# A Mamba-2 scan with an FFN on one core: increments of two pairs ahead of the state sums, two products ahead of y, and three unread products

## Chip, cores and metric

The kernel runs on one core of a Trainium2 chip. The metric is the device time in microseconds (us) of one execution; a number of executions give a median. Lower is better.

## What is computed

Two parts follow each other. The first is a Mamba-2 scan over 4 batches, 8 heads and 768 steps, in chunks of 32 in the reference; the second is a feed-forward layer over the 3072 rows of 256 that the scan gives.

```python
for c in range(nc):                       # scan, for each batch and head
    cum = np.cumsum(log_a[chunk])
    M = (C @ B.T) * exp(cum_i - cum_j) * causal
    y = M @ x + (C @ state) * exp(cum)
    state = exp(sum(la)) * state + sum_j B_j x_j exp(cum_last - cum_j)
h = y_rows @ w_in                         # 3072 x 256 by 256 x 2048
g = h / (1 + exp(-1.702 * h))
out = g @ w_out                           # 2048 x 256
```

All of it is in fp32. The weights come as 64-bit floats and are turned to fp32 in the kernel with integer and float operations (`fields`, `clamp`, `rounded`, `join`; `narrow` calls several of them).

## The kernel before

The 3072 rows are taken in six groups of 512. A group is two *pairs* (`p`), a pair is two stretches of 128 steps, and each such stretch has two sides of 64 steps; the kernel's chunk is one side. For a pair the scan does this:

- `decay` (VectorE) makes the decays L and the weighted B, Be; `turn_only` transposes B and C on TensorE into a PSUM bank `tp`, and ScalarE copies them out; `since_start` (VectorE, L546) makes CsT from the bank `tp`.
- `gain` (TensorE, L591) makes the four increments of the state of each pair in two PSUM banks, A0 and A1, that both pairs of a group share.
- `keep` (VectorE) first spreads a pair's increments out of A into the tile S (two operations, L610), and then adds the states up from side to side (up to four operations, L622), each of which reads the one before.
- `score` (TensorE, L560) makes C times B in the area `cb`; `weigh` (VectorE, L571) multiplies it into L.
- `finish` (TensorE) makes y: products of state and CsT (L649), products of L and x (L670), and the other state products. A tiny POOL operation stands between the first and the second set of state products. ScalarE then copies y out to yT (L694).

The scan of one group is woven into the feed-forward work of the one before. Group 0's hidden layer and projection are plain products: `half` (L729) and `hidden` (L715) make h, and `project_all` (L829) sums the output over 16 blocks, with other work given to it at numbered places: `at(in_project[0], 7, ...)` runs ahead of block 7's four products. From group 1 on both layers use seven products for 2 x 2 blocks instead of eight. A first-layer block j is written `j.1` to `j.7` (L787 into a bank X, L797 into a bank Y), `j.D` is VectorE's addition out of Y and the copies of X (L906), `j.S` and `j.T` are ScalarE's activations, and `j.3` needs `j.D` to have read Y. An additional VectorE addition follows `j.3`. `P` is one second-layer product into `acc` (L888). Second-layer products need mixes of the weights (`mix_w`, VectorE, L854) and of the activations (`mix_g`, L755).

The order on each engine is the order of the program text: `in_order` ties every instruction to the one before it on its engine. [...] PSUM banks come from a pool of four (`bank`), taken in turn: a new bank waits until the last reader of the one four before it is done. So Y of block 2 takes the bank that A0 had, and X and Y of the next blocks follow in turn. The tiles S come from a pool of three. SP issues nearly all transfers, in program order as well: the loads of later pairs (`load`), the spread of their decays (`spread`) and the stores.

In the first scan, `half(1, 0)` is the second set of hidden products of pair 0; it waits for a piece of `w_in` that VectorE joins (`join(1)`, L194). `half(0, 1)` is the first one of pair 1; it waits for yT. Between them on TensorE stands pair 1's y. VectorE's joins in turn wait for ScalarE's `clamp` (L172, L173), and ScalarE does these after its copy of y.

Of the kernel before, what the change touches and what calls it, by code (L numbers as in the profile page):

```python
# [16 lines left out]
P = 128  # L17
# [18 lines left out]
def kernel(  # L36
# [31 lines left out]
    nc = tc.nc  # L68
# [9 lines left out]
    NC = S // P  # L78
# [6 lines left out]
    PG = CG // 2  # L85
# [81 lines left out]
    def clamp(i):  # L167


        e = power[i]  # L170
        z = e.bitcast(FP32)
        nc.scalar.activation(z, e, AF.Relu, scale=-8.0, bias=edge[:, 0:1])  # L172
        nc.scalar.activation(e, z, AF.Relu, scale=-1.0, bias=edge[:, 1:2])  # L173
# [37 lines left out]
    def spread(p):  # L211

        if p - 2 in ra:
            ra[p] = ra[p - 2]
        else:
            ra[p] = words(f"a{p}").bitcast(FP32)[:, :2 * NH * H].rearrange(
                "p (k e) -> p k e", k=2)
        b, c = divmod(2 * p, NC)
        for i, side in enumerate(SIDES):
            nc.sync.dma_start(  # L220
                out=ra[p][side],
                in_=scratch[b, c:c + 2, i].rearrange("c h i -> c (h i)").unsqueeze(
                    0).to_broadcast([H, 2, NH * H]))
# [39 lines left out]
    ones = const.tile([P, P], FP32, name="ones")  # L263
# [33 lines left out]
    for k in range(2):  # L297
        t = cum[:, 2 * k:2 * k + 2].rearrange("p c s -> p (c s)")

        nc.vector.tensor_tensor_scan(  # L300
            out=t, data0=carry[:, 2 * k:2 * k + 2].rearrange("p c s -> p (c s)"), data1=t,
# [13 lines left out]
    def pick_a(p):  # L315
# [17 lines left out]
        out=same, in_=same, pattern=[[-N, NH], [0, D]], compare_op=ALU.is_ge,  # L333
        fill=0.0, base=0, channel_multiplier=1)
    nc.gpsimd.affine_select(
        out=same, in_=same, pattern=[[N, NH], [0, D]], compare_op=ALU.is_ge,
        fill=0.0, base=N - 1, channel_multiplier=-1)
# [7 lines left out]
        out=part, in_=same[:, :, 0].rearrange("p (r q) -> p q r", q=Q), op=ALU.add, axis=AX.X)  # L345
# [202 lines left out]
    def score(pairs, to=None):  # L548

        cb = (area(f"cb{pairs[0]}") if to is None else to).rearrange(  # L550
            "p r (k e) -> p r k e", k=2 * PG)
        for n, p in enumerate(pairs):
            s = st[p]
            BT, CT = s.pop("BT"), s.pop("CT")
            s["cb"] = cb[:, :, 2 * n:2 * n + 2]
            for k in range(2):
                for i, side in enumerate(SIDES):
                    for r in range(R):
                        rows = slice(32 * r, 32 * r + 32)
                        nc.tensor.matmul(  # L560
                            out=s["cb"][side, r, k].rearrange("p (q i) -> p q i", q=Q),
                            lhsT=BT[rows, k, side], rhs=CT[rows, k, :, side],
                            start=True, stop=True, tile_position=(32 * r, H * i),
                            skip_group_check=True)

    def weigh(p, ks=(slice(0, 2),)):

        Lv = Ls[p].rearrange("p k r q i -> p k r (q i)")
        cb = st[p]["cb"].rearrange("p r k e -> p k r e")
        for k in ks:  # L570
            nc.vector.tensor_tensor(out=Lv[:, k], in0=Lv[:, k], in1=cb[:, k], op=ALU.mult)  # L571
# [3 lines left out]
    def last_chunk(p, m):  # L575

        return (4 * p + m + 1) % (2 * NC) == 0

    def gain(pairs):

        A = [bank(f"A{pairs[0]}_{i}")[:, :2 * len(pairs) * Q * D].rearrange(
            "p (k e) -> p k e", e=Q * D) for i in range(2)]
        for n, p in enumerate(pairs):
            Be = BE.pop(p)
            for k in range(2):
                for r in range(R):
                    heads = slice(Q * r, Q * r + Q)
                    for i, side in enumerate(SIDES):
                        if last_chunk(p, 2 * k + i):
                            continue  # L590
                        nc.tensor.matmul(  # L591
                            out=A[i][32 * r:32 * r + 32, 2 * n + k],
                            lhsT=Be[side, k, heads].rearrange("p h n -> p (h n)"),
                            rhs=rx[p][side, k, heads].rearrange("p h d -> p (h d)"),
                            start=True, stop=True, tile_position=(H * i, 32 * r),
                            skip_group_check=True)
            increment[p] = [t[:, 2 * n:2 * n + 2] for t in A]

    def keep(p, ms=range(4)):

        b, c = divmod(2 * p, NC)
        if 0 in ms:
            state[p] = ssd.tile([P, 4, HB * D], FP32, tag="S", name=f"S{p}", bufs=3)
        new = state[p]
        ms = [m for m in ms if not last_chunk(p, m)]
        for i in range(2):
            ks = [m // 2 for m in ms if m % 2 == i]
            if ks:
                k, n = ks[0], len(ks)
                nc.vector.tensor_tensor(  # L610
                    out=new.rearrange("p (k s) (b e) -> p s k b e", s=2, b=HB // Q)[
                        :, i, k:k + n],
                    in0=increment[p][i][:, k:k + n].unsqueeze(2).to_broadcast(
                        [P, n, HB // Q, Q * D]),
                    in1=own.rearrange("p (b q) d -> p b (q d)", q=Q).unsqueeze(1).to_broadcast(
                        [P, n, HB // Q, Q * D]), op=ALU.mult)
        for m in ms:
            if 2 * c + m > 0:
                k, i = divmod(m, 2)
                old = new[:, m - 1] if m else state[p - 1][:, 3]  # L620
                e = i * H + H - 1
                nc.vector.scalar_tensor_tensor(  # L622
                    out=new[:, m], in0=old, scalar=since[b][:, c + k, e:e + 1],
                    in1=new[:, m], op0=ALU.mult, op1=ALU.add)
# [92 lines left out]

        nc.scalar.activation(gT[g, j][:, i], h, AF.Silu, scale=GELU_SCALE)

    def half(j, t):  # L720

        if t == 0:
            block(0, j)
        h = bank(f"h0_{j}_{t}").rearrange("p (i e) -> p i e", i=2)
        cols = slice(t * HT, (t + 1) * HT)
        for i in range(2):
            f = 2 * j + i
            for k in range(NK):
                nc.tensor.matmul(out=h[:, i], lhsT=w_in[:, k, f * P:(f + 1) * P],  # L729
                                 rhs=yT[0][:, k, cols] if t else early_y[:, k],  # L730
                                 start=(i == 0 and k == 0), stop=(i == 1 and k == NK - 1),
                                 skip_group_check=True)
        nc.scalar.activation(gT[0, j][:, :, cols], h, AF.Silu, scale=GELU_SCALE)
# [283 lines left out]
    keep(1, (0,))  # L1017
    join(1)
    keep(1, (1, 2))
    half(1, 0)  # L1020
    weigh(1)
    load(PG)
    spread_rows(1)
# [6 lines left out]
    def at(places, i, *work):  # L1030
        places.setdefault(i, []).extend(work)
# [10 lines left out]
    for i, k in ((2, 1), (3, 3), (4, 4), (5, 6)):  # L1042
# [13 lines left out]
    at(in_project[0], 2, lambda: clamp(8), lambda: decay(PG + 1), lambda: clip_rows(1),  # L1056
       lambda: decay_rows(1), lambda: turn(PG + 1))
    at(in_project[0], 4, lambda: narrow(8))
    at(in_project[0], 6, lambda: clamp(9), lambda: gain(pairs))
    at(in_project[0], 7, lambda: score(pairs), lambda: keep(PG), lambda: keep(PG + 1),  # L1060
       lambda: weigh(PG), lambda: weigh(PG + 1))
    at(in_project[0], 9, lambda: narrow(9))
    at(in_project[0], 11, lambda: finish(pairs))
# [4 lines left out]
    for k, i in enumerate((9, 13)):  # L1068
# [4 lines left out]

    later = n, n + 1
    at(after, "H0", lambda: decay(n), lambda: decay(n + 1), lambda: turn(n), lambda: turn(n + 1))
    at(after, "H1", lambda: gain(later), lambda: score(later), lambda: keep(n),
       lambda: keep(n + 1), lambda: weigh(n), lambda: weigh(n + 1), lambda: spread(3 * PG))
    assert [b for b in range(NB) if 3 * CG <= b * NC < 4 * CG] == [2]


    for f in range(NF):
        if f >= 4:
            hidden(0, f)
        elif f % 2:
            half(f // 2, 1)
        for do in in_hidden[0].get(f, []):
            do()
    project_all(0, in_project[0])
# [8 lines left out]
    def run(g, steps, products=(), **do):  # L1097


        products = iter(products)  # L1100
        for step in steps.split():
            if step == "P":
                product(*next(products))
            elif step in do:
                do[step]()
            else:
                j, i = step.split(".")
                first(g, int(j), i)
        assert next(products, None) is None
# [11 lines left out]
    def ahead(g, p=None):  # L1121

        pairs = (p, p + 1) if p else ()
        for k in pairs:
            turn_only(k)
        if pairs:
            gain(pairs)
        for k in pairs:
            since_start(k)
        mix_y(g)  # L1130
        for k in pairs:
            keep(k)

    def more_loads():
        load(p + 1)
        spread(p + 1)

    run(1, "2.1 3.1 2.5 2.6 3.6 2.2 2.7 3.5 3.7 3.2 2.D 2.4 3.D 3.4 2.S 3.S y L 2.3 2.T 3.3 3.T",
        y=lambda: finish(later), L=more_loads)
    mix_w(0)  # L1140
    for j in range(2):
        mix_g(1, j)
    run(1, "4.1 P P 4.6 P P 4.7 P 4.5 P 4.2 P 4.D", seven(1, 0))
# [97 lines left out]
```

## Time and profile before

| what | us |
|---|---|
| median of 4 runs | 370.53 (370.14 to 370.73) |
| the profiled execution, its time | 370.6 |
| the profiled execution, its span from the first to the last instruction | 368.8 |
| TensorE busy | 359.4 |
| VectorE busy | 251.0 |
| ScalarE busy | 150.7 |

The chain of work that ended last is, by the page, TensorE for 75% of the span and VectorE for 11%. A TensorE product of fp32 is two records in the trace, each with a weight load of its own. Here is the timeline as the profile tells it: the first scan lies in the first 25 us, group 0's hidden layer ends at about 52 us and its projection at about 87 us, with the scan of group 1's pairs inside it (A at 62.9, y at 74.4). Group 1's first hidden blocks follow, then A of group 2's pairs at 94.4 and their y at 102.6. From about 108 us on, both layers' products stand close together, and the scans of later groups stand between them (y at 160.5, 216.8 and 273.0).

A timeline line reads: start, length, engine, line and operation, what it writes and reads, how many instructions were merged, and in brackets the idle time ahead of it on its engine with what ended it ("issue" where the profile shows nothing that it waited for).

### The profile page before, as it was taken

How to read it: one execution, taken by the hardware profiler on the slowest of the kernel's cores; microseconds unless marked ns; L12 is line 12 of the kernel's file. 1: busy time of each engine (PE TensorE's matmuls, PEld its weight loads, DVE VectorE, ACT ScalarE, POOL GpSimd, SP SyncE). 2: the span in 40 equal slices, each digit the busy share in tenths (PEclk: the TensorE clock that was granted, in tenths of full speed). 3: DMA queues.
4: the chain of work that ended last, by engine and by line, in shares of the span. 5: the costliest groups of instructions: out<-in, count | busy, mean ns of one | idle time of the engine just before them, and what ended most of it. 6: DMA issues, size and time to landing. Idle time of an engine off the chain costs nothing.

```text
span 368.8 us, 8716 instructions
## 1 busy us (share of the span) xinstructions
PE 359.4 (97%) x3734; PEld 309.0 (84%) x3734; DVE 251.0 (68%) x472; ACT 150.7 (41%) x341; POOL 12.0 (3%) x42
## 2 busy tenths in 40 slices
PE   8989999999999999999999999999999999999995
PEld 4764468886679999889999989999988999989995
DVE  5989979997738999568577466577474355374353
ACT  5759553212442333444333444333435331453320
POOL 4310000000000000000000000000000000000000
PEclk9999999999999999999999999999999999999999
DMA  9997689045863210076200052000010000010001
GB/s 152 220 367 128 210 190 146 4 127 107 147 107 47 63 38 2 2 140 91 59 2 2 0 103 73 0 2 2 1 60 2 0 3 0 2 57 2 0 2 57
DMA packets 86029, 25.03 MB, mean 68 GB/s; under 512 B 76136, under 2 KB 79464, under 8 KB 85992
## 3 DMA queue, kind: packets, MB, share of 16 engines
q1 hardware_dynamic: 83544, 24.09, 29.7%
q10 hardware_dynamic: 2448, 0.39, 0.6%
q8 instruction: 29, 0.48, 0.6%
q14 instruction: 8, 0.07, 0.1%
HBM read 21.23 MB, written 3.24 MB: 66 GB/s over the span
## 4 chain that ended last, share of the span: by engine, by line
PE 75%; DVE 11%; issue 8%; SPq 2%; DMA 1%; ACT 1%; POOL 0%; ACTq 0%; DVEq 0%
PE acc L888 31%; PE X L787 16%; PE Y L797 12%; PE o L829 5%; PE y L649 3%; PE y L670 2%; PE h L715 2%; DVE p L188 2%; SPq L123 2%; PE cb L560 1%; DVE m L177 1%; PE tp L514 1%; DVE p L161 1%; PE A L591 1%; DVE m L164 1%
## 5 line engine op out<-in xcount | busy, mean ns | idle before, releaser
L888 PEld LDWEIGHTS acc<-mw,mg 128*128 128x128 f32 x480 | 67.5, 191 | 4.2
L888 PE MATMUL acc<-mw,mg 128*128 128x128 f32 x480 | 69.2, 275 | 0.0
L792 ACT ACTIVATE ac<-X 128x256 f32<-128x256 f32 x76 | 29.1, 383 | 81.1 <-PE X L787 80.6
L906 DVE TENSOR_TENSOR gT<-Y,ac 128x512 f32<-128x512 f32 x38 | 26.1, 690 | 48.7 <-PE Y L797 36.0
L764 ACT ACTIVATE gT<-gT 128x512 f32<-128x512 f32 (+1 forms) x76 | 39.4, 520 | 36.4 <-DVE gT L906 35.8
L888 PEld LDWEIGHTS acc<-w_out,gT 128*128 128x128 f32 x320 | 44.1, 191 | 2.5
L787 PE MATMUL X<-my,mi 128*128 128x256 f32 x152 | 45.7, 383 | 0.1
L888 PE MATMUL acc<-w_out,gT 128*128 128x128 f32 x320 | 45.2, 275 | 0.0
L906 DVE TENSOR_TENSOR gT<-Y,b 128x256 f32<-128x256 f32 x38 | 16.0, 421 | 34.4 <-PE Y L797 34.3
L829 PE MATMUL o<-w_out,gT 128*128 128x256 f32 x128 | 28.8, 381 | 0.0
L715 PE MATMUL h<-yT,w_in 128*128 128x512 f32 x64 | 28.5, 595 | 0.2 <-DVE w_in L194 0.2
L755 DVE TENSOR_TENSOR mg<-gT 128x512 f32<-128x512 f32 x40 | 27.3, 682 | 0.0
L829 PEld LDWEIGHTS o<-w_out,gT 128*128 128x128 f32 x128 | 23.9, 190 | 3.4 <-issue 0.2
L787 PEld LDWEIGHTS X<-my,mi 128*128 128x128 f32 x152 | 24.2, 191 | 1.7 <-ACT ac L792 0.3
L888 PEld LDWEIGHTS acc<-mw,gT 128*128 128x128 f32 x160 | 23.0, 191 | 2.2 <-DVE mw L854 0.4
L888 PE MATMUL acc<-mw,gT 128*128 128x128 f32 x160 | 24.4, 277 | 0.0
L888 PEld LDWEIGHTS acc<-w_out,mg 128*128 128x128 f32 x160 | 23.1, 191 | 1.4
L888 PE MATMUL acc<-w_out,mg 128*128 128x128 f32 x160 | 24.0, 275 | 0.0
L715 PEld LDWEIGHTS h<-yT,w_in 128*128 128x128 f32 x64 | 11.8, 190 | 14.1 <-issue 12.2
L797 PE MATMUL Y<-my,mi 128*128 128x256 f32 x76 | 22.8, 382 | 0.6 <-DVE S L610 0.5
L787 PE MATMUL X<-yT,w_in 128*128 128x256 f32 x76 | 22.9, 385 | 0.1
L787 PE MATMUL X<-my,w_in 128*128 128x256 f32 x76 | 22.8, 384 | 0.0
(137 smaller groups left out, 524.4 us busy)
## 6 DMA issues: line engine op xcount, KB each, us to landing
a<-scratch SPq DMA_DIRECT2D x18, 256.0 KB
bits<-in_moe_w_out_dram SPq DMA_DIRECT2D x4, 1024.0 KB
x<-in_x_dram SPq DMA_DIRECT2D x24, 128.0 KB
out_dram<-c SPq DMA_DIRECT2D x9, 256.0 KB
bits<-in_moe_w_in_dram SPq DMA_DIRECT2D x4, 512.0 KB
bits<-in_moe_w_in_dram SPq DMA_DIRECT2D x2, 1024.0 KB
b<-in_B_dram SPq DMA_DIRECT2D x24, 64.0 KB
c<-in_C_dram SPq DMA_DIRECT2D x22, 64.0 KB
```

Source lines behind the costliest of these rows:

```text
L123: (queue if dst is rc else nc.sync).dma_start(out=dst[p][:, k], in_=src[b, :, sl, :].rearrange("h s d -> s h d"))
L188: nc.vector.scalar_tensor_tensor(out=p2, in0=hi, scalar=0x80000000, in1=p2, op0=ALU.bitwise_and, op1=ALU.bitwise_or)
L649: nc.tensor.matmul(out=y[i][:, t, 2 * n + k], lhsT=old[rows], rhs=st[p]["CsT"][rows, k, SIDES[i]], start=begin(i, range(HB)), stop=False, ...
L715: nc.tensor.matmul(out=h, lhsT=w_in[:, k, f * P:(f + 1) * P], rhs=yT[g][:, k], start=(k == 0), stop=(k == NK - 1))
L755: nc.vector.tensor_tensor(out=t[:, 0:2], in0=B[:, :, 1], in1=B[:, 0], op=ALU.subtract)
L764: nc.scalar.activation(o, i, AF.Silu, scale=GELU_SCALE)
L787: nc.tensor.matmul(out=s["X"], lhsT=lhsT, rhs=rhs, start=i == "1", stop=i == "4", skip_group_check=True)
L792: nc.scalar.activation(copy, s["X"], AF.Copy)
L797: nc.tensor.matmul(out=o, lhsT=lhsT, rhs=rhs, start=s.pop("new", False), stop=i != "5", skip_group_check=True)
L829: nc.tensor.matmul(out=o[k // 2][:, k % 2], lhsT=gT[g, f // 2][:, f % 2, k * P:(k + 1) * P], rhs=w_out[:, f], start=(f == 0 and k % 2 == 0 ...
L888: nc.tensor.matmul(out=acc[g][0][i][:, cols], lhsT=h[:, cols], rhs=w, start=(j == 0 and i in (0, 2, 5, 6) and k == 0), stop=(j == NF // 2 ...
L906: nc.vector.tensor_tensor(out=o, in0=v, in1=w, op=ALU.add)
```

## The change

Five edits. `keep` is split into `part_of` (the increments out of A) and `add_up` (the sums), and `keep_both` does the first for both pairs and then the second for both. It takes the place of two calls of `keep` in group 0's projection, after group 1's first hidden blocks, and in `ahead`. `gain(pairs)` moves in group 0's projection from place 6 to place 7, so four products of block 6 now come before it. In group 1's first stretch, products `2.3` and `3.3` and the activations after them come ahead of `y`, and `mix_w(0)` goes from the end of that stretch to a place ahead of `2.3`. `half` can put products of ones into its own bank ahead of its real ones, which overwrite them: two ahead of `half(1, 0)`, one ahead of `half(0, 1)`. The operations that are computed and read are the same; the order on TensorE, VectorE and ScalarE changes, that on POOL and SP does not.

```diff
--- before.py
+++ after.py
@@ -598,7 +598,17 @@
 
     def keep(p, ms=range(4)):
 
-        b, c = divmod(2 * p, NC)
+        part_of(p, ms)
+        add_up(p, ms)
+
+    def keep_both(pairs):
+
+        for p in pairs:
+            part_of(p, range(4))
+        for p in pairs:
+            add_up(p, range(4))
+
+    def part_of(p, ms):
         if 0 in ms:
             state[p] = ssd.tile([P, 4, HB * D], FP32, tag="S", name=f"S{p}", bufs=3)
         new = state[p]
@@ -614,8 +624,12 @@
                         [P, n, HB // Q, Q * D]),
                     in1=own.rearrange("p (b q) d -> p b (q d)", q=Q).unsqueeze(1).to_broadcast(
                         [P, n, HB // Q, Q * D]), op=ALU.mult)
+
+    def add_up(p, ms):
+        b, c = divmod(2 * p, NC)
+        new = state[p]
         for m in ms:
-            if 2 * c + m > 0:
+            if 2 * c + m > 0 and not last_chunk(p, m):
                 k, i = divmod(m, 2)
                 old = new[:, m - 1] if m else state[p - 1][:, 3]
                 e = i * H + H - 1
@@ -717,12 +731,16 @@
 
         nc.scalar.activation(gT[g, j][:, i], h, AF.Silu, scale=GELU_SCALE)
 
-    def half(j, t):
+    def half(j, t, fill=0):
 
         if t == 0:
             block(0, j)
         h = bank(f"h0_{j}_{t}").rearrange("p (i e) -> p i e", i=2)
         cols = slice(t * HT, (t + 1) * HT)
+
+        for i in range(fill):
+            nc.tensor.matmul(out=h[:, i], lhsT=ones, rhs=ones.unsqueeze(1).to_broadcast([P, 2, P]),
+                             start=True, stop=True, skip_group_check=True)
         for i in range(2):
             f = 2 * j + i
             for k in range(NK):
@@ -1017,7 +1035,7 @@
     keep(1, (0,))
     join(1)
     keep(1, (1, 2))
-    half(1, 0)
+    half(1, 0, 2)
     weigh(1)
     load(PG)
     spread_rows(1)
@@ -1056,8 +1074,8 @@
     at(in_project[0], 2, lambda: clamp(8), lambda: decay(PG + 1), lambda: clip_rows(1),
        lambda: decay_rows(1), lambda: turn(PG + 1))
     at(in_project[0], 4, lambda: narrow(8))
-    at(in_project[0], 6, lambda: clamp(9), lambda: gain(pairs))
-    at(in_project[0], 7, lambda: score(pairs), lambda: keep(PG), lambda: keep(PG + 1),
+    at(in_project[0], 6, lambda: clamp(9))
+    at(in_project[0], 7, lambda: gain(pairs), lambda: score(pairs), lambda: keep_both(pairs),
        lambda: weigh(PG), lambda: weigh(PG + 1))
     at(in_project[0], 9, lambda: narrow(9))
     at(in_project[0], 11, lambda: finish(pairs))
@@ -1073,8 +1091,8 @@
 
     later = n, n + 1
     at(after, "H0", lambda: decay(n), lambda: decay(n + 1), lambda: turn(n), lambda: turn(n + 1))
-    at(after, "H1", lambda: gain(later), lambda: score(later), lambda: keep(n),
-       lambda: keep(n + 1), lambda: weigh(n), lambda: weigh(n + 1), lambda: spread(3 * PG))
+    at(after, "H1", lambda: gain(later), lambda: score(later),
+       lambda: keep_both(later), lambda: weigh(n), lambda: weigh(n + 1), lambda: spread(3 * PG))
     assert [b for b in range(NB) if 3 * CG <= b * NC < 4 * CG] == [2]
 
 
@@ -1082,7 +1100,7 @@
         if f >= 4:
             hidden(0, f)
         elif f % 2:
-            half(f // 2, 1)
+            half(f // 2, 1, f == 1)
         for do in in_hidden[0].get(f, []):
             do()
     project_all(0, in_project[0])
@@ -1128,16 +1146,15 @@
         for k in pairs:
             since_start(k)
         mix_y(g)
-        for k in pairs:
-            keep(k)
+        if pairs:
+            keep_both(pairs)
 
     def more_loads():
         load(p + 1)
         spread(p + 1)
 
-    run(1, "2.1 3.1 2.5 2.6 3.6 2.2 2.7 3.5 3.7 3.2 2.D 2.4 3.D 3.4 2.S 3.S y L 2.3 2.T 3.3 3.T",
-        y=lambda: finish(later), L=more_loads)
-    mix_w(0)
+    run(1, "2.1 3.1 2.5 2.6 3.6 2.2 2.7 3.5 3.7 3.2 2.D 2.4 3.D 3.4 2.S W 2.3 3.S 3.3 2.T 3.T y L",
+        y=lambda: finish(later), W=lambda: mix_w(0), L=more_loads)
     for j in range(2):
         mix_g(1, j)
     run(1, "4.1 P P 4.6 P P 4.7 P 4.5 P 4.2 P 4.D", seven(1, 0))
```

## The prediction, made before the changed kernel was run

> **What bounds the kernel now.** I read the page's shares first, then the waits by engine, then the TensorE timeline in the windows that the diff touches, and last VectorE's and the DMA queues' in the same windows.
>
> ```profile
> PE 359.4 (97%) x3734; PEld 309.0 (84%) x3734; DVE 251.0 (68%) x472; ACT 150.7 (41%) x341; POOL 12.0 (3%) x42
> ...
> q8 instruction: 29, 0.48, 0.6%
> ```
>
> TensorE is busy 97% of a span of 368.8 us. Its ends are modelled, so the question is not the 3% but where the starts of its groups stand further apart than their work. A change here can win only at such places. The diff touches three. The first, in the projection of group 0 (start us, length us, engine, line, operation; the bracket is the idle time before and its releaser):
>
> ```profile
> 62.86 0.30 PE L591 MATMUL A<-x,Be 64*32 64x64 f32 x2
> 63.50 0.78 PE L591 MATMUL A<-x,Be 64*32 64x64 f32 x54 [0.35 <-DVE CsT L546]
> 64.20 1.99 PE L829 MATMUL o<-w_out,gT 128*128 128x256 f32 x8
> 66.13 1.21 PE L560 MATMUL cb<-CT,BT 32*64 32x128 f32 x64
> 67.27 7.17 PE L829 MATMUL o<-w_out,gT 128*128 128x256 f32 x32
> ```
>
> The increments A (`gain`) start, then stop for a VectorE operation that frees their bank. Eight output records stand between A and the scores. The second place is group 1's first products and its y:
>
> ```profile
> 94.43 0.82 PE L591 MATMUL A<-x,Be 64*32 64x64 f32 x56
> 95.18 1.21 PE L560 MATMUL cb<-CT,BT 32*64 32x128 f32 x64
> 96.32 1.13 PE L787 MATMUL X<-yT,w_in 128*128 128x256 f32 x4
> 97.95 0.67 PE L797 MATMUL Y<-my,mi 128*128 128x256 f32 x2 [0.50 <-DVE S L610]
> ...
> 102.55 1.53 PE L649 MATMUL y<-CsT,S 64*128 64x64 f32 x16
> ...
> 106.68 0.67 PE L649 MATMUL y<-CsT,S 64*128 64x64 f32 x9 [0.61 <-issue]
> 107.28 1.13 PE L797 MATMUL Y<-yT,mi 128*128 128x256 f32 x4
> 108.25 0.59 PE L787 MATMUL X<-yT,w_in 128*128 128x256 f32 x2
> ```
>
> Here 0.50 us go to a bank that `keep` (L610) still reads, and 0.61 us to "issue", nothing the profile shows as a wait. VectorE in the same stretch has no gap, so it is next in line:
>
> ```profile
> 97.39 0.62 DVE L610 TENSOR_TENSOR S<-A,own 128x256 f32<-128x256 f32 x2
> ...
> 98.95 2.35 DVE L571 TENSOR_TENSOR L<-L,cb 128x1024 f32<-128x1024 f32 x2
> 101.21 1.28 DVE L906 TENSOR_TENSOR gT<-Y,ac 128x512 f32<-128x512 f32 x2
> ```
>
> The third place is the first scan, where the unread products go:
>
> ```profile
> 20.67 1.97 PE L729 MATMUL h<-y,w_in 128*128 128x256 f32 x8 [1.03 <-DVE w_in L194]
> ...
> 25.34 3.72 PE L729 MATMUL h<-yT,w_in 128*128 128x256 f32 x16 [0.74 <-ACT yT L694]
> ```
>
> [...] 29 packets of 0.48 MB[...] in the stretch from 103.5 to 104.5 us the only DMA is one such packet, at about 104.0, and the "issue" idle of 0.61 ends at 106.68. A y of two pairs has 320 TensorE records in some 3.5 us (L649 and L670)[...]. I read the idle as a late block; that is an inference. [...] The granted clock from 15 to 26 us is 1.00 with idle of at most 1.03 us, so the unread products have no clock to win in this trace. [...]
>
> **The change part by part.** The sums are made on the profiled execution: 370.6 us, of which the span is 368.8. The median of the runs is 370.53, 0.07 less.
>
> *`gain(pairs)` from place 6 to place 7 of group 0's projection.* Before, from A's start to the output products after the scores is 67.27 - 62.86 = 4.41 us: A 1.34, eight output records 1.93, scores 1.14. The 32 records after that take 7.10 us to y's start at 74.37, so one record is (7.10 - 1.93) / 24 = 0.215 and eight are 1.72; the other 0.21 of a visit is the switch from and to the small products. After it, the eight records extend the run ahead of A (1.72), A runs without the bank wait and straight into the scores as at 94.43 (0.75), scores 1.14: 3.61. That is 0.80 us less. VectorE reads A only at 68.10 (first L610), and A would be done at about 65.4, so nothing is later there. What is late next: y wants the weighed L, whose two L571 end at 73.84 on VectorE; y would start at 73.6 and reach the second pair's part after 1.0 us of state products and half of L670's 1.4, at 75.3. Covered by 1.4 us. Taken: -0.80, between -0.5 and -0.85.
>
> *`keep_both`.* Same operations, both pairs' increments (L610) before the sums (L622). The last reader of the bank is then done after four L610, 1.2 us after 95.29, instead of at 97.81. Y would start when its turn comes, at 96.32 + 4 x 0.215 + 0.10 = 97.3: 0.65 earlier. It is not kept whole: VectorE's row ends no earlier. The sums no longer overlap with an independent operation, some 0.1 us (rows of 0.38 apart against 0.34), so the two L906 "D" operations run 101.3 to 102.6. Groups 2 and 3 have the same edit in `ahead`; there no TensorE wait names L610, and VectorE is not the bound: 0.
>
> *Products 2.3 and 3.3, and `mix_w(0)`, ahead of y.* Before, y had to wait for ScalarE to empty both X banks (L764, 102.11 and 0.81 long); products 2.3 and 3.3 now fill that. They wait for D of their block: 2.3 starts at 102.05, 3.3 at 102.65, y at 103.2. Queued behind the two waits on TensorE is y alone, and behind y ScalarE's copy of yT. y without a stall takes 3.6 us (group 2: 160.53 to 164.01, 3.48, for four records fewer). Before it took 4.73: 0.25 for ScalarE and 0.88 around the "issue" gap. [...] About 20 records more stand ahead of it in the stream (12 of the unread products, 8 of the two moved), so 0.45 more of y follows the gap: 0.6 + 0.45, and X of block 4 starts at 107.4 instead of 108.25: -0.85. Bounds: with no gap 106.8 (-1.45); with the block as late after y's start as before, 108.4 (+0.15). Then two small terms that cancel: X's second product waits for a ScalarE copy that stands behind yT, +0.2; and the weight mixes (L854) are done before y's end, so the 0.4 us that the acc weights waited for them fall to 0, half of it on the path, -0.2. `mix_w(0)` delays the additions of 2.3 and 3.3 by four rows of 0.42, to 105.1; their reader, ScalarE's T, is needed much later. The loads L stay behind y and keep their place on SP's queue.
>
> *Unread products.* Three products of two records, 3 x 0.43 us. The first two lie in the 1.03 us that end with w_in (0.86 plus 0.10), the third in the 0.74 us that end with yT (0.43 plus 0.10). 0 us while that cover lasts. If it goes, they stand on the chain y -> yT -> p (L172) -> w_in and cost up to 1.3. [...]
>
> *Moved blocks later.* The same 20 records shift every later block. In group 2 the block that was first used right after y (164.6) is now wanted inside its last part. Its packet ended early enough by some 0.2 us to 1 us: +0.15, between 0 and 0.5.
>
> Sum: -0.80 - 0.85 + 0.15 = -1.5 us. 370.6 - 1.5 = 369.1 for the profiled execution; as a median 370.53 - 1.5 = 369.0.
>
> **Rivals.** (a) The gap at the block goes wholly, for y no longer waits between its first products[...]: -0.80 - 1.45 = -2.2, 368.3. For it: groups 2 to 4 have no such gap in y. Against: there y has other waits ahead. (b) Only the first edit counts: the gap stays as late after y's start as before, and 2.3 and 3.3 wait as long as they save; with a gap of 0.4 in group 2, -0.4: 370.1. For it: VectorE's row is closed from 95.29 to 102.5. (c) Slower: a late block in the first scan. y of pair 1 starts at 22.56, DMA is full there (367 GB/s in 15 to 26 us), and the 8 records of the first fill push the block's end 8 records ahead, onto the first products of y. A wait there is passed on whole: y, yT, p (VectorE idles 1.33 for it at 26.68), w_in, h. It decides from 1.5 us on; a packet that comes 3 us late gives 372.0. Against: before it was in time, and 8 records are 0.2 us. (d) The edit doesn't do what it says, Y's bank being held by another reader: then only the 0.65 is missing, of which D takes 0.5 anyway; 369.2, within the forecast.
>
> **How the numbers follow.** The forecast with (d) 0.56, (a) 0.16, (b) 0.19, (c) 0.09. The forecast's own bounds (-2.0 to -0.9) with (a) and most of (b) give 368.2 to 370.2. What the measurement can tell from no change is 0.2%, 0.74 us, so faster means below 369.8: all of (a), nearly all of the forecast and a little of (b), 0.73; same 0.18; slower 0.09.
>
> **What would show it.** A without a bracket and straight into cb, some 3.6 us from the added output products' start to the next o: the first term. Y at 97 without a DVE L610 bracket, then small brackets <-DVE gT L906 before the moved Y products: the second. One gap "issue" in y, of 0.2 to 0.8, and X of block 4 about 1.6 us earlier than 108.25 (0.8 and 0.85): the third. No change of h's starts at 20.67 and 25.34 shows the unread products free. Wrong would be: h later than these, a gap "issue" of over 1 us in any y, or Y products that wait over 1 us for D.

## The result, and the profile after

| | before | after |
|---|---|---|
| median of the comparison, us | 371.02 (63 runs, 369.38 to 374.92) | 369.43 (44 runs, 368.28 to 374.24) |
| ratio after / before, 95% interval | | 0.9958 (0.9941 to 0.9975) |
| a second comparison, us | 370.75 (65 runs) | 369.53 (22 runs) |
| its ratio | | 0.9968 (0.9941 to 0.9995) |
| profiled execution, time and span | 370.6, 368.8 | 369.54, 367.7 |

The change makes the kernel 1.6 us faster, where 1.5 was forecast. In part of the runs TensorE is at half clock for a few us (granted 0.50 for 3.41 us in one trace, for 10.24 in three), which makes them about 1.5 to 5 us longer, so the median of the runs with a mean granted clock of 0.998 or more, called "at full clock", stands beside the median of all. In the second comparison it is 370.20 before (45 of 65 runs) and 369.28 after (16 of 22): 0.92 us.

First the page of the kernel after, its busy times and its instruction queue:

```profile
PE 358.7 (98%) x3740; PEld 309.2 (84%) x3740; DVE 250.9 (68%) x472; ACT 151.1 (41%) x341; POOL 12.1 (3%) x42
...
q8 instruction: 29, 0.48, 0.5%
```

Six matmuls more than before, for the three unread products are two each; the other engines have the same work. TensorE's busy time hardly moves, so all of the gain lies in idle time and in modelled ends. TensorE's timeline of the kernel after at the first place:

```profile
64.87 0.79 PE L591 MATMUL A<-x,Be 64*32 64x64 f32 x56
65.59 1.21 PE L560 MATMUL cb<-CT,BT 32*64 32x128 f32 x64
66.72 7.24 PE L847 MATMUL o<-w_out,gT 128*128 128x256 f32 x32
73.90 1.11 PE L663 MATMUL y<-CsT,S 64*128 64x64 f32 x14
```

A has no bracket, comes whole, and goes straight into cb. Before, A was split by a wait of 0.35 and left by eight output records. The second place, the same view of the same kernel:

```profile
93.96 0.82 PE L591 MATMUL A<-x,Be 64*32 64x64 f32 x56
...
95.85 1.13 PE L805 MATMUL X<-yT,w_in 128*128 128x256 f32 x4
96.81 0.59 PE L815 MATMUL Y<-my,mi 128*128 128x256 f32 x2
...
101.61 1.30 PE L815 MATMUL Y<-yT,mi 128*128 128x256 f32 x4 [0.31 <-DVE gT L924]
102.83 1.11 PE L663 MATMUL y<-CsT,S 64*128 64x64 f32 x16
103.87 1.47 PE L684 MATMUL y<-L,x 64*32 64x64 f32 x126
106.01 0.27 PE L684 MATMUL y<-L,x 64*32 64x64 f32 x2 [0.68 <-issue]
106.21 1.11 PE L663 MATMUL y<-CsT,S 64*128 64x64 f32 x16
107.25 0.70 PE L805 MATMUL X<-yT,w_in 128*128 128x256 f32 x2
...
110.25 0.60 PE L805 MATMUL X<-my,mi 128*128 128x256 f32 x2
```

Y's bracket of 0.50 on `keep` is gone. In its place stands 0.31 ahead of product 2.3, which waits for D. The stop named "issue" is still there, 0.68 against 0.61, and not at the same operation: it stood between two L649 products, and now stands nine matmuls earlier, inside the L products (142 of y's matmuls ahead of it, before 151). VectorE in the same stretch shows why 2.3 waits:

```profile
94.82 1.28 DVE L620 TENSOR_TENSOR S<-A,own 128x256 f32<-128x256 f32 x4 [1.68 <-PE A L591]
...
98.60 2.35 DVE L571 TENSOR_TENSOR L<-L,cb 128x1024 f32<-128x1024 f32 x2
100.87 1.28 DVE L924 TENSOR_TENSOR gT<-Y,ac 128x512 f32<-128x512 f32 x2
```

All four increments come first and free the bank at 96.1, but the D additions (L924) begin no earlier for it: 6.91 us after A starts, 6.78 before. The timeline of the first scan after, with the unread products (L742):

```profile
18.62 1.03 PE L742 MATMUL h<-ones 128*128 128x256 f32 x4
20.93 1.99 PE L747 MATMUL h<-y,w_in 128*128 128x256 f32 x8 [1.29 <-DVE w_in L194]
...
24.83 0.70 PE L742 MATMUL h<-ones 128*128 128x256 f32 x2
25.64 3.72 PE L747 MATMUL h<-yT,w_in 128*128 128x256 f32 x16
```

They lie in the two waits that were there before. Last, y of group 2, where before no line of y had a bracket (from 160.53 to 164.01):

```profile
159.26 1.10 PE L663 MATMUL y<-CsT,S 64*128 64x64 f32 x14
160.29 1.48 PE L684 MATMUL y<-L,x 64*32 64x64 f32 x128
161.70 0.89 PE L663 MATMUL y<-CsT,S 64*128 64x64 f32 x12
162.85 0.32 PE L663 MATMUL y<-CsT,S 64*128 64x64 f32 x2 [0.26 <-issue]
163.10 0.70 PE L805 MATMUL X<-my,mi 128*128 128x256 f32 x2
```

This y takes 3.84 instead of 3.48 us: a new stop. To compare two traces, times are counted from TensorE's first product of L366 (`ab<-X`, in group 0's hidden layer; 39.76 before, 40.04 after), since the first scan varies by some tenths from run to run. These are the lines of before that the comparison needs, in the order of time:

```profile
39.76 0.69 PE L366 MATMUL ab<-X,ones 32*64 32x256 f32 x16
74.37 1.11 PE L649 MATMUL y<-CsT,S 64*128 64x64 f32 x14
111.54 0.60 PE L787 MATMUL X<-my,mi 128*128 128x256 f32 x2
160.53 1.10 PE L649 MATMUL y<-CsT,S 64*128 64x64 f32 x14
164.01 0.70 PE L787 MATMUL X<-my,mi 128*128 128x256 f32 x2
```

| place | time from `ab<-X`, before | after | difference |
|---|---|---|---|
| y of group 1's first pairs starts | 34.61 | 33.86 | -0.76 |
| X of block 4 starts (108.25, 107.25) | 68.49 | 67.21 | -1.29, so -0.53 more |
| second `X<-my,mi` behind group 1's y starts (111.54, 110.25) | 71.79 | 70.21 | -1.58, so -0.82 more in all |
| length of group 2's y | 3.48 | 3.84 | +0.36 |
| end of the span | 329.05 | 327.69 | -1.37 |

A second trace of the changed kernel (`r_after`) agrees within 0.1 us up to the second `X<-my,mi`, has a longer stop in group 2's y, and ends at -0.94.

### The profile page after: what moved, and what is told of

The parts are those of the page before. It is cut to its first block, busy times and chain, and to the rows that moved or that the text cites. A ratio compares the mean times of both kernels' runs of the same rounds, so it can differ in the third digit from the quotient of the medians.

```text
span 367.7 us, 8727 instructions
## 1 busy us (share of the span) xinstructions
PE 358.7 (98%) x3740; PEld 309.2 (84%) x3740; DVE 250.9 (68%) x472; ACT 151.1 (41%) x341; POOL 12.1 (3%) x42
## 4 chain that ended last, share of the span: by engine, by line
PE 83%; issue 6%; DVE 5%; SPq 2%; DMA 2%; ACT 1%; POOL 0%
PE acc L906 31%; PE X L805 16%; PE Y L815 12%; PE o L847 8%; PE h L729 6%; PE y L663 3%; SPq L123 2%; PE y L684 2%; PE cb L560 2%; DMA bits<-in_moe_w_in_dram 1%; PE tp L514 1%; PE A L591 1%; DVE p L188 1%; DVE m L177 1%; DMA az<-in_a_dram 1%
## 5 line engine op out<-in xcount | busy, mean ns | idle before, releaser
L924 DVE TENSOR_TENSOR gT<-Y,ac 128x512 f32<-128x512 f32 x38 | 26.1, 690 | 53.7 <-PE Y L815 36.0
L924 DVE TENSOR_TENSOR gT<-Y,b 128x256 f32<-128x256 f32 x38 | 15.9, 421 | 28.8 <-PE Y L815 28.8
L815 PE MATMUL Y<-yT,mi 128*128 128x256 f32 x76 | 22.8, 383 | 0.3 <-DVE gT L924 0.3
```

The lines of the kernel that those rows point to most:

```text
L815: nc.tensor.matmul(out=o, lhsT=lhsT, rhs=rhs, start=s.pop("new", False), stop=i != "5", skip_group_check=True)
L924: nc.vector.tensor_tensor(out=o, in0=v, in1=w, op=ALU.add)
```

## Experiments

Theory: the gain comes from the first two terms, -0.8 each, less what the additional TensorE records cost by moving instruction blocks (a block: what one packet of the queue q8 brings, as I read it). Rivals: one edit does it all; or the unread products matter by TensorE's clock. "From `ab<-X`" is the time to the span's end, against 329.05 before.

**One part of the change at a time.**

`e1_gain_only` moves the increments and nothing else:

```diff
-    at(in_project[0], 6, lambda: clamp(9), lambda: gain(pairs))
-    at(in_project[0], 7, lambda: score(pairs), ...
+    at(in_project[0], 6, lambda: clamp(9))
+    at(in_project[0], 7, lambda: gain(pairs), lambda: score(pairs), ...
```

> Only gain moved from place 6 to 7. My theory (the edits act at separate places, each worth what its waits and switches were): A runs without the VectorE bracket and straight into cb, output products on either side are one visit fewer, y of group 1 starts 0.75 us earlier against the first scan's end; time 0.6 to 0.8 us under before (ratio about 0.998). The number of TensorE records ahead of each later y is unchanged, so the 'issue' gap in group 2's y stays absent and the one after A at 94 stays at the same place in y. Rival (this edit is the whole change, the others cancel): 1.5 us under before, ratio 0.996. Rival (hidden anyway): no difference.

Measured: 369.83 against 370.71, ratio 0.9985 (0.9964 to 1.0005); at full clock 369.56 against 370.34, -0.78; from `ab<-X` -0.91. The interval alone does not exclude no gain, but the traces and the full clock agree on some 0.8. The lines are those of the first place above:

```profile
64.02 0.79 PE L591 MATMUL A<-x,Be 64*32 64x64 f32 x56
64.74 1.21 PE L560 MATMUL cb<-CT,BT 32*64 32x128 f32 x64
65.88 7.23 PE L829 MATMUL o<-w_out,gT 128*128 128x256 f32 x32
```

`e2_keep_only` has only `keep_both`, in its three places:

```diff
-       lambda: keep(PG), lambda: keep(PG + 1),
+       lambda: keep_both(pairs),
...
-        for k in pairs:
-            keep(k)
+        if pairs:
+            keep_both(pairs)
```

> Only keep_both, at all its places. My theory: the Y product at about 98 loses its bracket from VectorE L610 (0.65 us with what lies around it), and as y still comes before products 2.3 and 3.3 here, nothing waits for D, so all of it stays: 0.6 us under before, ratio 0.998. Rival (VectorE is the bound in this stretch and takes it back): under 0.2 us.

Measured: 369.85, ratio 0.9971 (0.9952 to 0.9991); at full clock -0.62; from `ab<-X` -0.68. Alone the edit keeps the whole of its 0.65: y starts 7.37 us after A, before 8.12.

`e3_y_only` moves 2.3, 3.3 and `mix_w(0)` ahead of y:

```diff
-    run(1, "... 2.S 3.S y L 2.3 2.T 3.3 3.T", ...)
-    mix_w(0)
+    run(1, "... 2.S W 2.3 3.S 3.3 2.T 3.T y L", ..., W=lambda: mix_w(0), ...)
```

> Only the order in group 1: 2.3, 3.3 and mix_w(0) ahead of y. My theory: the Y bracket at 98 stays, 2.3 and 3.3 find D done, y starts as late as in the whole change, block 4's X starts some 0.5 us earlier and the acc weights wait no more: about 0.8 us by the end of that stretch. So keep_both adds hardly anything on top of this edit, and the two alone sum to more than together. The 8 records that now stand ahead of y push the instruction block's end forward; in group 2 y then gets an 'issue' gap of about 0.4. Net 0.4 to 0.8 under before. Rival (additive edits): this one alone gives under 0.3 us.

Measured: 371.11, ratio 0.9994 (0.9967 to 1.0022); one more execution of the same kernel, `e8_y_look`, gave 371.14. Neither the median nor its cause was foreseen. 9 of the 14 runs lie below full clock; the five at full clock have a median of 368.95, -1.39, and from `ab<-X` the trace shows -1.46, of which 0.46 are a shorter stop in group 1's y. The median hid a gain because of the clock in the first scan, which this edit doesn't touch; that so many of its runs are below may be chance. The stop of 0.4 that was expected in group 2's y is not there: that y takes 3.48 us, as before.

> Another look at the kernel with only y moved, 9 of whose 14 timed runs had a mean clock of 0.995 or less. Clock theory: if this profile is one of those, TensorE's matmuls of some 3.4 us in the first scan run at half speed after an idle of about 1 us, and the span is 1.7 us longer for each such spell. Rival (the lower mean clock lies at the start or the end of the span): no stretch in the first scan with doubled matmuls.

This execution caught it. Its windows (columns: stretch, its length, busy time and instructions of each engine, granted clock, share and rate of DMA), and its TensorE timeline there:

```profile
15.00:21.00 6.00, 3.84 (x106) 2.89 (x87) 5.09 (x11) 4.43 (x9) 1.48 (x2) 1.00 1.02 314
21.70:25.10 3.40, 3.40 (x29) 2.36 (x34) 3.36 (x8) 0.60 (x1) 0.00 (x0) 0.50 1.03 395
26.00:36.00 10.00, 9.26 (x37) 5.84 (x36) 7.40 (x11) 8.22 (x12) 0.00 (x0) 1.00 0.82 185
```

```profile
16.78 1.99 PE L729 MATMUL h<-y,w_in 128*128 128x256 f32 x8
20.93 3.04 PE L729 MATMUL h<-y,w_in 128*128 128x256 f32 x8 [2.16 <-DVE w_in L194]
23.90 1.12 PE L649 MATMUL y<-CsT,S 64*128 64x64 f32 x8
24.95 0.90 PE L670 MATMUL y<-L,x 64*32 64x64 f32 x64
25.79 0.66 PE L649 MATMUL y<-CsT,S 64*128 64x64 f32 x8
27.19 1.13 PE L729 MATMUL h<-yT,w_in 128*128 128x256 f32 x4 [0.74 <-ACT yT L694]
```

Set this beside the kernel after, whose h starts at 20.93 as well: its products take 1.99, not 3.04, its y's first ones 0.66, not 1.12, and the next h starts at 25.64, not 27.19. The wait for w_in was 2.16 long without unread products; in the trace of before, whose first h starts 0.86 us later, it was 1.03. Half clock from 21.7 to 25.1 cost 1.55 us.

`e4_fill_only` has only the unread products, which are overwritten by the real ones:

```diff
+        for i in range(fill):
+            nc.tensor.matmul(out=h[:, i], lhsT=ones, rhs=ones..., start=True, stop=True)
...
-    half(1, 0)
+    half(1, 0, 2)
...
-            half(f // 2, 1)
+            half(f // 2, 1, f == 1)
```

> Only the three unread products. My theory: the products themselves cost nothing (they lie in waits of 1.03 and 0.74 us that end when they did), but their 12 records stand in front of every later y: the 'issue' gap appears in group 2's y, 0.3 to 0.5 us, and the one in group 1's later y moves some 10 records ahead. 0 to 0.4 us over before. Rival (they keep TensorE's clock up): no lower clock in any run and 0.3 us or more under before. Rival (they are late for what stands behind them): h starts after w_in and yT by more than 0.1 us and the first scan ends 0.3 to 1.3 us later.

Measured: 371.19, ratio 1.0004 (0.9983 to 1.0025); at full clock 371.12, which is 0.78 slower; from `ab<-X` +0.79. Only 1 of 14 runs was below full clock, against 21 of 59 of the kernel before in that comparison. So the products cost and win at once. The cost is not where they stand. Group 1's y takes 5.00 instead of 4.73 us, and group 2's, 140 us later, 4.16 instead of 3.48:

```profile
161.12 1.10 PE L649 MATMUL y<-CsT,S 64*128 64x64 f32 x14
162.16 1.48 PE L670 MATMUL y<-L,x 64*32 64x64 f32 x128
163.57 0.89 PE L649 MATMUL y<-CsT,S 64*128 64x64 f32 x12
165.03 0.32 PE L649 MATMUL y<-CsT,S 64*128 64x64 f32 x2 [0.57 <-issue]
```

Nothing in this stretch was edited. What differs is how many records come before it.

**The whole change, with other unread products.** `e5_no_fill` is the changed kernel without them (`half(1, 0)` and `half(f // 2, 1)` as before).

> The whole change without the three unread products. Block theory (12 records fewer ahead of every y): group 2's y has no 'issue' gap, the one in group 1's y comes 10 records later; from the first scan's end (the fan of X, L366) to the span's end 0.4 to 0.7 us less than in the whole change. Clock theory (the unread products keep TensorE from a spell of half clock in the first scan; seen in 25 of 117 runs without them at a mean clock of 0.994 to 0.995, in none of 58 with them): such runs are back in about one of five. Median then within 0.5 us of the whole change, either way. Rival (the unread products do nothing but shift): no run at 0.995.

Measured: 370.07 against 370.96, ratio 0.9965 (0.9938 to 0.9992); at full clock 368.19 against 369.99, -1.80. Group 2's y is whole again (3.48), and from `ab<-X` the trace ends at -2.32, 0.96 less than the change, where 0.4 to 0.7 was expected. 12 of 22 runs were below full clock, but only 3 of them at 0.993 to 0.995, the expected kind; 8 were at 0.986 or less. (The 25 of 117 runs named above are 24.)

`e6_wide_fill` makes the first two unread products one of double width. The same TensorE time is spent, with four records fewer:

```diff
-        for i in range(fill):
-            nc.tensor.matmul(out=h[:, i], lhsT=ones, rhs=ones... [P, 2, P],
+        for i in range(min(fill, 1)):
+            nc.tensor.matmul(out=h if fill == 2 else h[:, i], lhsT=ones,
+                             rhs=ones... [P, 2 * fill, P],
```

> The whole change with the two first unread products made one of double width: the same 0.86 us of TensorE, 4 records instead of 8. Block theory: group 2's y starts 4 records earlier against the block's end, which is where it had no gap in the run with only y moved; the 0.48 us gap goes or halves, the one in group 1 stays. Clock theory: no run at 0.994 to 0.995. So 0.3 to 0.5 us under the whole change. Rival (the gap in group 2 has to do with waits, not with the count of records): it stays at 0.48.

Measured: 368.40, ratio 0.9921 (0.9897 to 0.9945), at full clock 368.35 (20 of 22 runs, none at 0.993 to 0.995). Group 2's y takes 3.60 us, 0.12 of stop being left.

`e7_gain_y_wide` is that kernel with `keep` pair by pair, as before the change.

> gain moved, the order of group 1 changed, the wide unread products, and no keep_both. If the release of A's bank was worth nothing once 2.3 and 3.3 stand ahead of y (they wait for D, which VectorE ends at the same time either way): the 0.65 us bracket at Y returns, the wait for D goes, y starts when it does in the whole change, and [...]the gap in group 1's y is about 0.4 instead of 0.9. From the first scan's end to the span's end 0.6 to 1.0 us less than in the whole change. Rival (the edits add up): 0.6 us more than it.

Measured: 368.26 (9 runs, all at full clock), ratio 0.9914 (0.9887 to 0.9942). From `ab<-X` it ends at -2.11, 0.74 less than the change, as expected; the edits don't add up.

**All of them in one comparison.** `e9_gain_y_only` is the same again without any unread product.

> The changed kernel once more, beside the two that were faster in other comparisons. Theory (every edit's worth is read in TensorE's record count and in half-clock spells): 369.4 us as before, ratio 0.996. Rival (the wide-product version was only luckier in its comparison): all of this group lie within 0.3 us of each other.

> The changed kernel with its first two unread products as one of double width (the same time of unread work, four records fewer). Theory: 0.5 to 1.0 us under the changed kernel of the same comparison, since no instruction block falls into group 2's y; ratio 0.992 to 0.994. Rival: the same time as the changed kernel within 0.3 us.

> The gain moved, 2.3 and 3.3 ahead of y, and the wide unread product, but keep in its old place pair by pair. Theory: D isn't late for 2.3, which gives back what keep_both saves: within 0.3 us of the wide version, 368.3 us. Rival (keep_both keeps its 0.65 us): 0.5 us or more slower than the wide version.

> The same without any unread product. Theory (unread products win only by the clock): the fastest runs as fast as those of the version with the wide unread product, within 0.4 us, but a third or more of the runs with a mean granted clock of 0.995 or less, against few with it; median 0.3 to 1.0 us higher. Rival (the unread products win nothing): the median is equal or lower by up to 0.5 us, and the clocks are spread alike.

| kernel (before: 370.75) | median, us | ratio, interval | median at full clock (before: 370.20) | runs below full clock |
|---|---|---|---|---|
| `r_after`, the change | 369.53 | 0.9968 (0.9941 to 0.9995) | 369.28 | 6 of 22 |
| `r_wide` | 368.68 | 0.9925 (0.9889 to 0.9961) | 368.59 | 3 of 12 |
| `r_gain_y_wide` | 369.16 | 0.9960 (0.9931 to 0.9989) | 368.91 | 6 of 22 |
| `e9_gain_y_only` | 370.23 | 0.9973 (0.9949 to 0.9996) | 368.69 | 13 of 22 |

Four things follow.

The wide version beats both kernels: 2.6 and 2.1 us faster than before in its two comparisons, 0.85 faster than the change in the one that has both. The intervals of the two ratios overlap there, so its lead over the change rests also on the earlier ratio (0.9921 against the change's 0.9958) and on the traces. From `ab<-X` its two end at -2.15 and -2.45, the change's two at -1.37 and -0.94. More of this lies in group 1's y (3.82 and 3.71 us long, against 4.42 and 4.50) than in group 2's (3.92 and 3.60 up to the next X, against 3.84 and 4.21). Both places in `r_wide`, where group 2's y is whole and what is left of its stop comes after it:

```profile
105.53 1.11 PE L663 MATMUL y<-CsT,S 64*128 64x64 f32 x16 [0.26 <-issue]
...
160.89 1.10 PE L663 MATMUL y<-CsT,S 64*128 64x64 f32 x14
162.36 0.59 PE L806 MATMUL X<-my,mi 128*128 128x256 f32 x2 [0.37 <-issue]
```

The stop in group 2 had been expected to be gone, not 0.37. In `e6_wide_fill`, the same kernel, the timeline has no bracket there. A shorter stop in group 1's y was not foreseen.

`keep_both` is worth nothing once 2.3 and 3.3 stand ahead of y. From A's start to y's start `r_wide` takes 102.75 - 93.88 = 8.87 us and `r_gain_y_wide`, without it, 103.28 - 94.42 = 8.86. The wait only moves, as the second kernel's timeline shows:

```profile
97.93 0.67 PE L802 MATMUL Y<-my,mi 128*128 128x256 f32 x2 [0.50 <-DVE S L610]
...
102.32 1.03 PE L802 MATMUL Y<-yT,mi 128*128 128x256 f32 x4
103.28 1.11 PE L649 MATMUL y<-CsT,S 64*128 64x64 f32 x16
```

The medians don't rank the two: the one without it is 0.14 lower in the first comparison and 0.48 higher in the second, where within 0.3 was expected; from `ab<-X` their second traces end at -2.12 and -2.15. One kernel's gain at full clock differed by 0.4 us between comparisons (-1.73 and -1.29 for this one), so smaller differences than that are not read here.

The unread products win by the clock alone: without them `e9_gain_y_only` is as fast at full clock (its fastest run is 367.64, that of `r_wide` 367.53), but 13 of 22 runs fall below, and its median is 1.07 above that of `r_gain_y_wide`, the same kernel with them.

And the stops named "issue" go by record count, not by operation. The traces' TensorE records (weight loads, matmuls and semaphore records) were counted from the first. This table has the distance in us from the record before to two of them, whatever operation they are; within one part of y such distances are at most about 0.06, and 0.1 to 0.2 where one part follows another and at a first X after y:

| kernel | record 2497 | record 3777, and what it is |
|---|---|---|
| before | 0.88 | 0.21, X |
| `e1_gain_only`, `e2_keep_only`, `e3_y_only`, `e8_y_look` | 0.80, 0.87, 0.42, 0.59 | 0.21, 0.16, 0.21, 0.21, X |
| `e5_no_fill`, `e9_gain_y_only` | 0.30, 0.95 | 0.21, 0.21, X |
| after, `r_after`, `e4_fill_only` | 0.89, 0.98, 1.04 | 0.48, 0.84, 0.80, y |
| `e6_wide_fill`, `r_wide` | 0.22, 0.33 | 0.13, 0.45, X |
| `e7_gain_y_wide`, `r_gain_y_wide` | 0.56, 0.55 | 0.00, 0.00, X |

The two numbers are 1280 records apart. The three unread products have twelve records, two matmuls and two weight loads each, and two semaphore records fall away with them. So group 2's y starts at record 3468 instead of 3458, and record 3777 is in it. With the wide product it starts at 3464, and 3777 is just behind it; without unread products it is further behind.

What ends such a stop can be read from the instruction packets (queue q8, 16 KiB each in the trace), which I take for TensorE's by their number: in the changed kernel one starts at 103.35, ahead of record 2497, and the fifth after it at 160.50, ahead of record 3777. 1280 records over five packets are 256 each. There are 29 packets in each trace, and 29 records 193, 449, and so on to 7361, each 256 behind the last. Here is one of the packets in the changed kernel, between 102.5 and 106 us in 40 slices:

```profile
DMA  0000000009000000000000000000000000000258
q8 instruction: 1, 0.02, 2.4%
```

It is the one of 103.35; record 2497 starts at 106.01. Taken in order, one packet for the block that begins one boundary later, no first record of a block starts less than 2.31 us after the start of its packet, in all 14 traces. The 19 stops of the table (all 14 at record 2497, and five at record 3777: the three in y and the two of `e6_wide_fill` and `r_wide`) end 2.31 to 2.70 us after it. I read these stops as TensorE waiting for its next block. Their length is then what is left of those 2.3 to 2.7 us when the block before is used up: 0.30 in `e5_no_fill`, whose packet starts 0.59 ahead of record 2241, and 0.95 in `e9_gain_y_only`, whose packet starts 0.13 behind it. That the packets carry the blocks in this order is inferred from the times, not shown by an experiment.

## Why the prediction was right, and where it was not

*The increments moved, -0.80:* right. -0.76 in the trace after, -0.78 at full clock alone. A stands whole, and nothing was late behind it.

*`keep_both`, 0.65 that "is not kept whole" for VectorE's row:* right in kind. Y starts 2.85 us after A (foreseen 2.87, before 3.52). Of the 0.65, D was to take 0.5; it takes all of it beside the moved products (8.87 us from A to y with the edit, 8.86 without). It is kept whole only when the edit is alone (`e2_keep_only`).

*2.3 and 3.3 ahead of y, -0.85 with the former:* right in sum, -0.82, but in part by luck. At X of block 4, which the term names, -0.53 is reached; the other -0.29 comes up to the second `X<-my,mi`, where two small terms were to cancel. The step put the end of the stop at about 106.35, since y's last wait was to end at 102.6 instead of 102.9; that the packet follows that wait was my estimate, and no trace shows it. Counted from A's start its packet came at 9.54 us before, and at 9.39 and 9.67 in the two traces after, so not earlier; y itself started 0.10 later than foreseen, and the stop stayed what it was (0.88 before, 0.89 and 0.98 after).

*Unread products, 0 us, as "the unread products have no clock to win in this trace":* the step that failed, although the sum stood. "In this trace" was true and was taken for all runs. The trace of before is at a clock of 1.0, but 60 of 170 runs of that kernel are below 0.998. Runs with a mean clock of 0.993 to 0.995, which fits one stretch of 3.4 us at half clock in 368 (`e8_y_look` has one of 3.41 and a mean of 0.995), were 30 of 170 for before (three comparisons), 20 of 102 for the five kernels without unread products, and 0 of 145 for the seven comparisons of kernels with them. Two other kinds are not removed: runs at 0.990 or 0.991 (8 of 170, 7 of 102 and 8 of 145) and at 0.986 or less (22, 19 and 22). Three traces caught the last kind. In `e9_gain_y_only` and in `e6_wide_fill`, which has an unread product, the half clock began at 13.9 and 14.3 us, ahead of the place of these products; in `e5_no_fill` it began at 22.4, behind a wait of 2.14 for w_in, where the unread products would stand.

*Moved blocks, +0.15 between 0 and 0.5:* right in kind, the size too small. In the trace before, record 3777 starts 3.07 us after its packet, as X and with no stop; after, it starts 2.34 us behind its packet, inside y, with the stop. The count was wrong as well: "the same 20 records shift every later block" takes in the eight of the two moved products, which had stood ahead of group 2 before, too. In `e3_y_only` group 2's y starts at record 3458, as before; the shift there is ten, by the unread products alone. Group 2's y became 0.36 longer in the trace after, but 0.73 in `r_after` (4.21) and 0.68 in `e4_fill_only` (4.16). Taking the full clock, the unread products cost the whole change 1.80 - 0.92 = 0.88 us (two comparisons, so within 0.4), and alone 0.78.

The two misses have opposite signs. At full clock the change is worth 0.9, and 1.8 without unread products. The share of runs at half clock falls with them from 12 of 22 to 18 of 66, and the medians come out alike (369.43 and 369.53 with them, 370.07 without, each in its own comparison). From `ab<-X` the change's two traces end at -1.37 and -0.94, so the sum of -1.5 was too large for a run at full clock. A forecast of the median by one trace at full clock was right here by that cancellation, which is luck.

*Rivals:* (a), the stop going wholly, did not happen. (b), the first edit alone, is excluded by the second place. (c), a late block in the first scan, did not occur in any trace: h starts 1.4 us after y's last part with the unread product (24.24 to 25.64) and without it (25.79 to 27.19), and record 705, the one such boundary in that y, is at most 0.05 us behind the record before it in all traces. (d) is excluded by the Y line.

## What to carry to other kernels

When a trace shows a stop named "issue", count the engine's records up to it in two kernels. If the count is the same and the operation isn't, as here at record 2497 in all 14 traces, a record added or removed ahead moves it to another operation, so look where it will land before adding filler; here four records fewer for the same time took it out of group 2's y. Then look for the instruction packet: what counted here is the time from its start to the first record of its block (2.31 us at least). Look at the granted clock of every run, not only of the profiled one, before saying that a wait has no clock to lose; and try edits that free the same wait together, since their gains did not add here (at full clock 0.78, 0.62 and 1.39 alone, 1.80 together).

## What the runs showed of the hardware that was not expected

The stop does not come at every block: of the 29 records that begin one, it stands at one in the trace before (2497) and at two in the trace after (2497 and 3777). Record 1729 lies in the y of group 1's first pairs, 1.9 to 2.15 us behind record 1473, and had no stop in any kernel (0.01 or less), while 2497 followed 2241 after 1.4 to 1.8 us of work with stops of 0.2 to 1.0, and 3777 followed 3521 after 2.0 us with stops of 0.5 to 0.8 where it lay in y. The packets tell them apart: that of 1729 starts 4.0 to 4.6 us ahead of its block, well ahead of record 1473, those of 2497 and 3777 near records 2241 and 3521, so that 256 small records are used up before the 2.3 us are over. No packet starts more than 293 records ahead of its block. What sets when a packet starts stays open: for 2497 it was between 0.73 us ahead of record 2241 and 0.13 behind it, and two executions of the changed kernel differ by 0.3. Other instruction lengths were not tried.

The half clock in `e8_y_look` was expected after an idle of about 1 us, and came after a wait of 2.16. In these traces the clock changes only at multiples of 3.41 us from its first change (in before from 7.14 to 368.95: 361.81 us, 106 times 3.413); such a stretch is called a step here. In the step just ahead of the half clock TensorE was busy for 1.25 us in `e8_y_look`, with its wait of 2.16, and for 1.42 in `e5_no_fill`, with 2.14. Steps with a wait of 1.03 (before) or 1.29 (after), 2.38 and 2.13 us busy, were not followed by it. Idle time doesn't explain the other two traces: in `e6_wide_fill` and `e9_gain_y_only` the step ahead was busy for 3.10 us, and before has such a step (3.11) without half clock behind it. The half clock lasted one step, 3.41 us, in `e8_y_look`, and three, 10.24 us, in the other three traces. These are the lines inside it of `e5_no_fill` and `e6_wide_fill`:

```profile
22.50:32.60 10.10, 9.36 (x95) 7.19 (x94) 6.36 (x13) 3.99 (x8) 0.34 (x2) 0.50 0.93 268
14.30:24.40 10.10, 10.10 (x154) 7.63 (x153) 9.09 (x21) 6.07 (x13) 1.40 (x3) 0.50 1.03 346
```

In the second TensorE's busy time is 10.10 of 10.10, so by the busy share alone it looks like a full engine.
